# Three feature tiles converted half by half, and the first tile's slot matrix made by one full-width product

## The chip, the cores and the metric

The kernel runs on one core of a Trainium2 chip. The time is the device time of one execution in microseconds. Where several runs are given, it is their median. One execution of the kernel before was also profiled; its span goes from the first instruction to the last and is a little shorter than its own time.

## What is computed

Three layers follow each other on 4 batches of 576 tokens (2304 tokens, model width 512): local attention with 8 heads of 64, a soft mixture of experts with 32 slots, and a feed-forward layer of 2048 features with a gated rectifier. The change touches the end of the second and the beginning of the third:

```python
    slot_out[e] = h @ w2[e]            # the soft mixture, 32 slots of 512
    x = c @ slot_out                   # c: 2304 x 32, the share of each token in each slot
    h = x @ w_in
    g = np.maximum(h, 0.0) + alpha * np.minimum(h, 0.0)
    return g @ w_out
```

w_in and w_out arrive as 64-bit floats, which the kernel itself turns into 32-bit ones on the chip.

## The kernel before, in words

**The order of the third layer.** x is never formed. As h = c @ (slot_out @ w_in), the kernel first multiplies the 32 slot rows by w_in and keeps the result split into a rounded part and a remainder (mpack); a product with cpack, the tokens' shares in the same split form, then gives h. The 2048 features are cut into 16 tiles of 128, f = 0 to 15, the tokens into three blocks r of 768. The table VISITS names the order in which blocks and tiles meet: block 0 with tile 0, block 1 with tiles 0 and 1, block 2 with tiles 0 to 2, block 0 with tiles 1 to 3, and so on. One meeting of a block and a tile is a step s; steps 0, 1 and 3 use tile 0, step 2 is the first with tile 1, step 5 with tile 2, step 8 with tile 3. A visit's six accumulators y (one PSUM bank each for 128 tokens) are copied out or added to what earlier visits left.

**soT.** The slot rows end up transposed in PSUM (tile st). At line 843 one ScalarE copy moves them to soT, 128 x 4 x 32: for each of four blocks of 128 of the model width (k), the 32 slots. The planned order below begins right behind it.

**Converting a tile (conv, lines 779 to 804).** One DMA brings the two weights of a tile, 1 MB of 64-bit words; w_in lies in the first half of the columns, w_out in the second. Step 0 takes the absolute value of the upper words on ScalarE (line 786). Steps 1 and 2 clamp and shift (VectorE, lines 788 and 790, one input each). Steps 3 and 4 bring in the sign and the lowest bits (VectorE, lines 793 and 796, two inputs each). Step 4 also makes SP issue the load of the tile that comes four later (load_one, line 248), for f from 2 on. Step 5 rounds w_out to wo_hi, step 6 leaves the remainder as wo_lo (line 803). For f > 0 all of 1024 columns go through steps 0 to 4 at once, as tasks c0 to c4, and c5 and c6 are on ScalarE and VectorE. Tile 0 is done in two halves of 512: its w_in before the planned order starts, its w_out as tasks d0 to d4, then c5 and c6 on VectorE.

**From a tile to h (lines 889 to 973).** m1(f) (line 892) multiplies soT with the tile's w_in, four products of 32 columns packed side by side into PSUM, one for each k, so that the four partial sums stand in four groups of 32 partitions. ms copies them to SBUF on ScalarE (line 419, shown as q_m<-hb). m2 (line 969) is a product with the constant sel_s that adds the four groups and writes the sum four times below each other. mp (ScalarE, line 419, mpack<-hb) rounds it into mpack, and m3 (VectorE, line 897) puts the remainder into its lower half.

**A step.** For each of two halves i of a block: h (line 903, TensorE), relu (ScalarE, line 1007), gate (VectorE, line 911), ghs, the rounded copy (ScalarE, line 419), gls, the remainder (GpSimd, line 1013). Then 18 products y (line 917): for six groups of 128 tokens ghs with wo_hi, ghs with wo_lo, gls with wo_hi. Evictions of y are copies on ScalarE (line 419) or additions on VectorE (line 925).

**Who sets the order.** Each engine works through its own queue in program order. The tasks above are put in order by a planner written in the kernel (plan and schedule, lines 86 to 193): a list scheduler that takes the task that can start earliest, by a table of costs (COST), and at equal starts the one with the smallest key. The keys come from the place at which a tile is first used (when) less a LEAD for each kind of task; a randomised search over 1500 rounds shifts keys and keeps an order if its planned end is not later. A task can have an earliest time; for steps 0 to 4 of tiles 1 to 5 it is 2.6 f + 1.6 us. The tasks of a tile are made here:

```python
            task(("m1", f), "pe", lambda f=f: m1(f), [dep("c4", f), dep("ms", f - 1)], k - LEAD["m1"])
            task(("ms", f), "act", lambda f=f: copy("act", ms[:, f % 2], mb[0]), [("m1", f), dep("m2", f - 2)],
                 k - LEAD["ms"])
            task(("m2", f), "pe", lambda f=f: mm(mb[1], lhsT=sel_s, rhs=ms[:, f % 2], start=True, stop=True),
                 [("ms", f), dep("m3", f - 1)], k - LEAD["m2"])
```

Until the first y can start, TensorE is kept running with products that nobody reads (warm, line 501): 2, 4 and 6 of them behind m1(0), m2(0) and the second h.

Of the kernel before, what the change touches and what calls it, by code (L numbers as in the profile page):

```python
# [10 lines left out]
F32 = mybir.dt.float32  # L11
# [8 lines left out]
B, H, S, D = 4, 8, 576, 64  # L20
NT, DM, NS, DFF, NE, EF = 2304, 512, 32, 2048, 8, 1024
# [11 lines left out]
          (1, 12, NF), (2, 14, NF))  # L33
NEXT = {f: f + 4 for f in range(2, NF - 4)}
PRE = (4, 5)


PERIOD = 4.3
# [2 lines left out]
            relu=(0.39, 0.52), gate=(0.53, 0.64), gh=(0.42, 0.54), gl=(1.3, 1.35), ms=(0.17, 0.3), mp=(0.17, 0.3),  # L41
            m3=(0.3, 0.32), copy=(0.48, 0.62), add=(0.66, 0.72), c0=(1.05, 1.18), c1=(0.95, 1.0), c2=(0.95, 1.0),
            c3=(1.65, 1.75), c4=(1.5, 1.6), c5=(0.52, 0.64), c6=(1.25, 1.35),
            d0=(0.6, 0.7), d1=(0.44, 0.5), d2=(0.44, 0.5), d3=(0.75, 0.8), d4=(0.72, 0.8),
            q=(0.75, 2.9), k=(0.75, 2.9), qq=(1.45, 3.6), v=(1.5, 3.7), vh=(0.75, 2.95), w=(2.7, 4.9), sm=(0.215, 0.4), s=(0.96, 1.15), max=(0.67, 0.7), sub=(0.69, 0.72), exp=(0.56, 0.66),
            sum=(0.69, 0.72), rec=(0.42, 0.46), norm=(1.04, 1.1), t=(0.44, 0.7), pv=(0.96, 1.25),
# [7 lines left out]
FROUNDS = 1500  # L54
MODE = dict(sm=128, t=128, x=128, dT=128, s=64, pv=64, lt=32, part=32)
LAND = 3.5
LEAD = dict(h=15, relu=14, gate=10, gh=8, gl=2, m1=34, ms=32, m2=30, mp=26, m3=25, c0=70, c1=66, c2=62, c3=58, c4=50, c5=24,
            c6=14, warm=60, pb=8)
# [125 lines left out]
def tile_kernel(ctx, tc, qk, v, phi, w1, w2, w_f, alpha, mask, out):  # L184
    nc = tc.nc
# [39 lines left out]
    eps_s = const.tile([128, 1], F32, name="eps_s")  # L225

    slotT = keep.tile([128, 4, NS], F32, name="slotT")
    soT = keep.tile([128, 4, NS], F32, name="soT")
    rinv = keep.tile([128, 1], F32, name="rinv")
    lts = keep.tile([96, B, 192], F32, name="lts")  # L230


    plan = []
# [183 lines left out]
    def copy(eng, out, in_):  # L417
        if eng == "act":
            nc.scalar.copy(out=out, in_=in_)  # L419
        elif eng == "dve":  # L420
            nc.vector.tensor_copy(out=out, in_=in_)
        else:
            nc.gpsimd.tensor_copy(out=out, in_=in_)
# [183 lines left out]
    with tc.manual_schedule():  # L607
# [34 lines left out]
        b = B - 1  # L642
# [197 lines left out]
        warm(2, st[:, 256:384])  # L840
        emit_st()
        warm(2, st[:, 256:384])
        nc.scalar.copy(out=soT, in_=st[:, 0:4 * NS].rearrange("p (k s) -> p k s", k=4))
        ex.close()


# [37 lines left out]
        def task(name, engine, fn, need, key, kind=None, ready=0.0):  # L884

            need = [n for n in need if n is not None]
            tasks[name] = (engine, fn, need, key, *COST[kind or name[0]], ready)

        def m1(f):
            w = fbuf[f % 4]  # L890
            for g in range(4):
                mm(mb[0][32 * g:32 * g + 32, :], lhsT=soT[:, g, :], rhs=w[:, 128 * g:128 * g + 128], start=True,  # L892
                   stop=True, skip_group_check=True)

        def m3(f):
# [53 lines left out]
        def dep(*n):  # L949
            return n if n in tasks else None  # L950

        for f in range(NF):
            k = when[f]
            if f > 0:
                landed = [("c4", x) for x in NEXT if NEXT[x] == f and x > 0]
                for i in range(7):
                    need = {0: landed + [dep("c6", f - 4), dep("m1", f - 4)], 5: [("c4", f)], 6: [("c5", f)]}
                    task((f"c{i}", f), "act" if i in (0, 5) else "dve", lambda f=f, i=i: conv(f, i),
                         need.get(i, [(f"c{i - 1}", f)]), k - LEAD[f"c{i}"], f"c{i}",
                         2.6 * f + 1.6 if f < 6 else 0.0)  # L960
            else:
                for i in range(5):
                    task((f"d{i}", 0), "dve" if i else "act", lambda i=i: conv(0, i, 1), [dep(f"d{i - 1}", 0)], -40, f"d{i}")
                task(("c5", 0), "dve", lambda: conv(0, 5), [("d4", 0)], -40, "c5")
                task(("c6", 0), "dve", lambda: conv(0, 6), [("c5", 0)], -2, "c6", 3.0)
            task(("m1", f), "pe", lambda f=f: m1(f), [dep("c4", f), dep("ms", f - 1)], k - LEAD["m1"])
            task(("ms", f), "act", lambda f=f: copy("act", ms[:, f % 2], mb[0]), [("m1", f), dep("m2", f - 2)],
                 k - LEAD["ms"])
            task(("m2", f), "pe", lambda f=f: mm(mb[1], lhsT=sel_s, rhs=ms[:, f % 2], start=True, stop=True),
                 [("ms", f), dep("m3", f - 1)], k - LEAD["m2"])  # L970
            task(("mp", f), "act", lambda f=f: copy("act", mpack[:, 128 * f:128 * f + 128], mb[1]), [("m2", f)],
                 k - LEAD["mp"])
            task(("m3", f), "dve", lambda f=f: m3(f), [("mp", f)], k - LEAD["m3"])
        seen, last_y = {}, {}
# [23 lines left out]
        for s, (v, r, f) in enumerate(steps):  # L998
            for i in range(2):
                k = when[s, i]  # L1000
                task(("h", s, i), "pe", lambda s=s, i=i: h_(s, i), [("m3", f), dep("gate", s - 1, i)], k - LEAD["h"])
                if (s, i) == (0, 1):
                    for j, (after, m) in enumerate(((("m1", 0), 2), (("m2", 0), 4), (("h", 0, 1), 6))):
                        task(("warm", j), "pe", lambda m=m: (y[0, 5] is None and bank(0, 5), warm(m, y[0, 5][:, 0:128])),
                             [after], -LEAD["warm"], "warm%d" % m)
                task(("relu", s, i), "act",
# [9 lines left out]

        def place(name):

            return {"h": name[-1], "relu": name[-1], "gate": name[-1], "m1": 0, "ms": 0, "m2": 1, "mp": 1, "m3": 1}.get(name[0])

        schedule(tasks, place, lambda name, x: LAND if name[0] == "c0" and x[0] == "c4" else 0.0, rounds=FROUNDS, spread=(3, 10, 30))

# [56 lines left out]
```

## Time and profile before

| what | value |
|---|---|
| median of three runs | 381.15 us (380.51 to 381.78) |
| the profiled execution, its own time | 381.29 us |
| its span | 379.5 us |
| TensorE busy in the span | 360.5 us (95%) |
| VectorE busy | 267.7 us (71%) |
| ScalarE busy | 216.5 us (57%) |
| GpSimd busy | 159.7 us (42%) |
| chain that ended last, by engine | TensorE 68%, DMA 14%, VectorE 10%, ScalarE 4% |

The profile calls the engines PE (TensorE; PEld is its weight load), DVE (VectorE), ACT (ScalarE), POOL (GpSimd) and SP. A line gives the output and input tile; small helpers such as the copy at line 419 stand for many tasks, told apart by their tiles. Tiles are named by the memory they lie in: feature tiles in conversion are pt_m and e_m, their raw weights q_m, xs_m or v_m, and both PSUM banks of h and of the slot products are hb. The busy shares are means over stages with different limits: attention and the loads of the experts' weights come before 139 us and the third layer after.

### The profile page before, as it was taken

Reading aid. Unit: us, or ns where it says so; the run is one execution under the profiler, and the core shown is the slowest. Engines: PE = TensorE matmul, PEld = TensorE weight load, DVE = VectorE, ACT = ScalarE, POOL = GpSimd, SP = SyncE. Lnnn points to the kernel's source line nnn. Section 1 sums busy time; section 2 is a strip of 40 time slices with the busy share of each in tenths; the row PEclk is TensorE's granted clock in tenths of the full one; section 3 lists DMA queues with packets and bytes.
Section 4 is the critical chain, followed back from the end, with each engine's and each line's share of the span. In section 5 each row is a group of like instructions: output and inputs, shape, how many; then the busy total and the mean of one; then the engine's idle time right before and its main releaser. Section 6 shows DMA issues by size and latency. Waiting matters only on the chain.

```text
span 379.5 us, 7885 instructions
## 1 busy us (share of the span) xinstructions
PE 360.5 (95%) x3108; PEld 269.6 (71%) x3108; DVE 267.7 (71%) x450; ACT 216.5 (57%) x470; POOL 159.7 (42%) x141
## 2 busy tenths in 40 slices
PE   7699999899999988799999999999999999999995
PEld 4486786766444446578778778888778877888884
DVE  5979989875237449999999989899786225224263
ACT  3568977484123238967884956755557435535450
POOL 5347666320000004546554566664545434633550
PEclk9999999999899999999999999999999999999999
DMA  8999999999999994233232333020000000003246
GB/s 300 417 415 373 374 394 418 408 369 422 419 419 415 416 422 198 68 139 126 111 113 90 131 112 111 9 104 0 3 0 1 3 0 0 2 0 107 62 140 191
DMA packets 15044, 74.01 MB, mean 195 GB/s; under 512 B 1920, under 2 KB 2320, under 8 KB 8992
## 3 DMA queue, kind: packets, MB, share of 16 engines
q1 hardware_dynamic: 14032, 71.80, 48.6%
q10 hardware_dynamic: 912, 1.64, 1.2%
q8 instruction: 24, 0.39, 0.4%
q14 instruction: 12, 0.10, 0.1%
q0 software_dynamic: 64, 0.07, 0.1%
HBM read 68.79 MB, written 4.72 MB: 194 GB/s over the span
## 4 chain that ended last, share of the span: by engine, by line
PE 68%; DMA 14%; DVE 10%; ACT 4%; issue 2%; POOL 0%; ACTq 0%; DVEq 0%; SPq 0%; POOLq 0%
PE y L917 49%; DMA w<-w 8%; PE hb L903 4%; DMA q_m<-qk 3%; PE pv L403 2%; PE si L485 2%; PE s L355 2%; DVE e_m L369 2%; PE h L714 1%; PE x L476 1%; DMA m_m<-mask 1%; DMA q_m<-w_f 1%; PE hb L892 1%; DVE l L376 1%; DVE m L366 1%
## 5 line engine op out<-in xcount | busy, mean ns | idle before, releaser
L1013 POOL TENSOR_TENSOR gls<-gs,ghs 128x384 fp32r<-128x384 f32 x96 | 116.1, 1224 | 162.9 <-ACT ghs L419 112.0
L917 PE MATMUL y<-wo_hi,ghs 128*128 128x512 f32 x289 | 90.8, 397 | 1.2 <-ACT ghs L419 0.9
L911 DVE SCALAR_TENSOR_TENSOR gs<-gs,beta_s,hb 128x384 f32<-128x384 f32 x96 | 56.5, 609 | 49.2 <-ACT gs L1007 45.8
L917 PE MATMUL y<-wo_hi,gls 128*128 128x512 f32 x289 | 87.5, 392 | 1.1 <-POOL gls L1013 1.1
L917 PE MATMUL y<-wo_lo,ghs 128*128 128x512 f32 x289 | 88.4, 392 | 0.0
L1007 ACT ACTIVATE gs<-hb 128x384 f32<-128x384 f32 x96 | 44.9, 495 | 45.5 <-PE hb L903 39.0
L917 PEld LDWEIGHTS y<-wo_hi,gls 128*128 128x128 f32 x289 | 54.1, 188 | 13.0 <-POOL gls L1013 1.7
L917 PEld LDWEIGHTS y<-wo_hi,ghs 128*128 128x128 f32 x289 | 53.3, 188 | 13.5 <-ACT ghs L419 2.4
L419 ACT CAST ghs<-gs 128x384 fp32r<-128x384 f32 x96 | 48.9, 518 | 22.3 <-DVE gs L911 21.6
L917 PEld LDWEIGHTS y<-wo_lo,ghs 128*128 128x128 f32 x289 | 54.0, 188 | 10.3
L903 PE MATMUL hb<-cpack,mpack 128*128 128x384 f32 x96 | 29.2, 342 | 1.7 <-DVE mpack L897 1.1
L385 POOL TENSOR_TENSOR e_m<-e_m,l 128x512 f32<-128x512 f32 x18 | 19.1, 1066 | 27.1 <-DVE l L381 18.0
L355 PE MATMUL s<-q_m 128*64 128x64 f32 x576 | 20.9, 224 | 2.7 <-DMA q_m<-qk 1.5
L355 PEld LDWEIGHTS s<-q_m 128*64 128x64 f32 x576 | 18.7, 138 | 5.5 <-issue 2.1
L903 PEld LDWEIGHTS hb<-cpack,mpack 128*128 128x128 f32 x96 | 17.9, 188 | 6.3 <-DVE mpack L897 1.3
L403 PEld LDWEIGHTS pv<-pt_m,v_m 128*64 128x64 f32 x576 | 18.2, 138 | 5.7 <-issue 3.0
L403 PE MATMUL pv<-pt_m,v_m 128*64 128x64 f32 x576 | 20.4, 224 | 1.6 <-issue 1.3
L419 ACT COPY pt_m<-t 64x512 f32<-64x512 f32 x35 | 20.2, 578 | 2.3 <-PE t L390 1.8
L717 ACT ACTIVATE v_m<-h,rinv 128x256 f32<-128x256 f32 x8 | 3.8, 474 | 22.4 <-PE h L714 22.4
L372 ACT ACTIVATE e_m<-e_m 128x512 f32<-128x512 f32 x18 | 11.2, 629 | 7.7 <-DVE e_m L369 7.6
L788 DVE TENSOR_SCALAR pt_m<-pt_m 128x1024 f32<-128x1024 f32 (+1 forms) x9 | 9.8, 1083 | 8.1 <-ACT pt_m L786 8.1
L366 DVE TENSOR_REDUCE m<-s 128x8 f32<-128x512 f32 x18 | 12.1, 671 | 2.2 <-PE s L355 2.2
(164 smaller groups left out, 512.1 us busy)
## 6 DMA issues: line engine op xcount, KB each, us to landing
w<-w SPq DMA_DIRECT2D x23, 1024.0 KB, 10.8
q_m<-qk SPq DMA_DIRECT2D x13, 576.0 KB, 6.8
q_m<-w_f SPq DMA_DIRECT2D x7, 1024.0 KB, 4.9
v_m<-w_f SPq DMA_DIRECT2D x7, 1024.0 KB, 4.8
v_m<-v SPq DMA_DIRECT2D x12, 576.0 KB, 7.8
q_m<-w SPq DMA_DIRECT2D x4, 1024.0 KB, 13.2
v_m<-w SPq DMA_DIRECT2D x2, 1024.0 KB, 14.8
q_m<-qk SPq DMA_DIRECT2D x4, 288.0 KB, 5.2
```

Source lines behind the costliest of these rows:

```text
L355: mm(s[r:r + 64, col:col + 64], lhsT=q_of(u)[:, 2 * o:2 * o + 64], rhs=keys(u, c, x), start=False, stop=True, skip_group_check=True)
L366: nc.vector.tensor_reduce(out=m, in_=by_key(s_[g]), op=ALU.max, axis=AX.X)
L372: nc.scalar.activation(out=es[g % 4], in_=es[g % 4], func=AF.Exp, scale=SCALE)
L385: nc.gpsimd.tensor_tensor(out=e, in0=e, in1=bc(e_[g, "l"], 128, 8, 64), op=ALU.mult)
L403: mm(pv[hs, n], lhsT=vv[u % 4][:, c, hs], rhs=pts[:, NBS * (g % 2) + n, h], start=True, stop=True, skip_group_check=True)
L419: nc.scalar.copy(out=out, in_=in_)
L788: nc.vector.tensor_scalar(out=t, in0=t, scalar1=2.0 ** -15, scalar2=FMAX, op0=ALU.max, op1=ALU.min)
L903: mm(hb[i], lhsT=mpack[:, 128 * f:128 * f + 128], rhs=cpack[:, t0:t0 + 384], start=True, stop=True)
L911: nc.vector.scalar_tensor_tensor(out=g, in0=g, scalar=beta_s[:, f:f + 1], in1=hb[i], op0=ALU.mult, op1=ALU.add)
L917: mm(y[steps[s][0], t][:, sl], lhsT=g, rhs=wo_hl[p == 1][:, f, sl], start=start, stop=stop, skip_group_check=True)
L1007: lambda s=s, i=i: nc.scalar.activation(out=half(gs, s, i, 4), in_=hb[i], func=AF.Relu, scale=-1.0),
L1013: lambda s=s, i=i: nc.gpsimd.tensor_tensor(out=half(gls, s, i, 6), in0=half(gs, s, i, 4), in1=half(ghs, s, i, 6).bitcast(F32), op=ALU.subt ...
```

## The change

soT becomes 128 x 4 x 4 x 32, each group of 32 slots written four times side by side, by ScalarE for the first two k and by VectorE for the other two. It shares its memory with lts, which nobody reads any more by then. For tile 0, m1 is four products of full width that accumulate in one place, mb[1]; ms and m2 of tile 0 are gone, and mp reads m1's result. Tiles 1 to 3 go through steps 0 to 4 in two halves of 512 columns, tasks i0 to i4 for w_in and c0 to c4 for w_out, the latter with keys later by 10 and never ahead of the same step of the first half; m1 waits for i4 only. c5 and c6 work as before. The load of the tile four later hangs on the second half. c6 of tile 0 has a later key than before, and c5 of tile 0 too. The warming products behind m1(0) and m2(0) are now four behind m1(0).

```diff
+SPLIT = (1, 2, 3)
...
+            m10=(0.9, 1.0),
...
-    soT = keep.tile([128, 4, NS], F32, name="soT")
     rinv = keep.tile([128, 1], F32, name="rinv")
-    lts = keep.tile([96, B, 192], F32, name="lts")
+    lts_m = keep.tile([128, B * 192], F32, name="lts")
+    lts = lts_m[0:96].rearrange("p (b c) -> p b c", b=B)
+    soT = lts_m[:, 0:16 * NS].rearrange("p (k r s) -> p k r s", k=4, r=4)
...
-        nc.scalar.copy(out=soT, in_=st[:, 0:4 * NS].rearrange("p (k s) -> p k s", k=4))
+        so = st[:, 0:4 * NS].rearrange("p (k o s) -> p k o s", k=4, o=1)
+        for i, eng in enumerate(("act", "dve")):
+            k = slice(2 * i, 2 * i + 2)
+            copy(eng, soT[:, k], so[:, k].to_broadcast([128, 2, 4, NS]))
...
         def m1(f):
             w = fbuf[f % 4]
-            for g in range(4):
-                mm(mb[0][32 * g:32 * g + 32, :], lhsT=soT[:, g, :], rhs=w[:, 128 * g:128 * g + 128], start=True,
+            for g in range(4 * (f == 0)):
+                mm(mb[1], lhsT=soT[:, g].rearrange("p r s -> p (r s)"), rhs=w[:, 128 * g:128 * g + 128], start=(g == 0), stop=(g == 3))
+            for g in range(4 * (f > 0)):
+                mm(mb[0][32 * g:32 * g + 32, :], lhsT=soT[:, g, 0], rhs=w[:, 128 * g:128 * g + 128], start=True,
                    stop=True, skip_group_check=True)
...
             if f > 0:
-                landed = [("c4", x) for x in NEXT if NEXT[x] == f and x > 0]
-                for i in range(7):
...
+                landed = [("c4", x) for x in NEXT if NEXT[x] == f and x > 0] + [dep("c6", f - 4), dep("m1", f - 4)]
+                at = 2.6 * f + 1.6 if f < 6 else 0.0
+            for i in range(5):
+                if f in SPLIT:
+                    task((f"i{i}", f), "dve" if i else "act", lambda f=f, i=i: conv(f, i, 0), [(f"i{i - 1}", f)] if i else landed,
+                         k - LEAD[f"c{i}"], f"d{i}", at)
+                h = 1 if f == 0 or f in SPLIT else None
+                need = [(f"c{i - 1}", f)] if i else landed if f else []
+                task((f"c{i}", f), "dve" if i else "act", lambda f=f, i=i, h=h: conv(f, i, h),
+                     need + [dep(f"i{i}", f)], (k - LEAD[f"c{i}"] if f else -40) + 10 * (f in SPLIT), f"d{i}" if h else f"c{i}", at if f else 0.0)
+            for i in (5, 6):
+                task((f"c{i}", f), "act" if i == 5 and f else "dve", lambda f=f, i=i: conv(f, i), [(f"c{i - 1}", f)],
+                     k - LEAD[f"c{i}"] if f else -60 + 20 * i, f"c{i}", 0.0 if f or i == 5 else 3.0)
+            task(("m1", f), "pe", lambda f=f: m1(f), [dep("i4" if f in SPLIT else "c4", f) if f else None, dep("ms", f - 1)], k - LEAD["m1"],
+                 "m1" if f else "m10")
+            if f > 0:
+                task(("ms", f), "act", lambda f=f: copy("act", ms[:, f % 2], mb[0]), [("m1", f), dep("m2", f - 2)],
+                     k - LEAD["ms"])
...
-                    for j, (after, m) in enumerate(((("m1", 0), 2), (("m2", 0), 4), (("h", 0, 1), 6))):
+                    for j, (after, m) in enumerate(((("m1", 0), 4), (("h", 0, 1), 6))):
```

## Rows read from the trace of the kernel before

**Rows 1.** Stretches: length, busy PE, PEld, DVE, ACT, POOL (count); clock, DMA share, GB/s.
```profile
151.90:153.10 1.20, 0.30 (x3) 0.11 (x2) 0.64 (x2) 1.20 (x5) 0.00 (x0) 1.00 0.00 0
...
157.98:159.05 1.07, 0.02 (x2) 0.01 (x1) 1.07 (x3) 1.07 (x3) 1.07 (x2) 1.00 0.00 0
...
165.00:180.00 15.00, 15.00 (x74) 12.14 (x74) 14.74 (x17) 10.86 (x26) 8.19 (x6) 1.00 0.40 141
...
240.00:375.44 135.44, 135.43 (x649) 111.00 (x647) 76.67 (x111) 69.99 (x151) 63.58 (x57) 1.00 0.13 40
```

**Rows 2.** TensorE's waits from 139.3 to 166 us (total, times, longest).
```profile
PE y L917 <- POOL gls L1013: 1.1, 1, 1.1
PE y L917 <- ACT ghs L419: 0.9, 1, 0.9
```

**Rows 3.** ScalarE in order of time, 139 to 168 us (start, us, ...).
```profile
139.25 0.27 ACT L843 COPY soT<-st 128x128 f32<-128x128 f32 x1 [1.69 <-PE st L501]
139.42 0.68 ACT L786 ACTIVATE pt_m<-q_m 128x512 f32<-128x512 f32 x1
...
140.91 0.27 ACT L419 CAST mpack<-hb 128x128 fp32r<-128x128 f32 x1 [0.58 <-PE hb L969]
...
143.33 0.87 ACT L1007 ACTIVATE gs<-hb 128x384 f32<-128x384 f32 x2 [1.10 <-PE hb L903]
...
152.47 0.57 ACT L419 CAST ghs<-gs 128x384 fp32r<-128x384 f32 x1
...
163.12 1.16 ACT L786 ACTIVATE e_m<-q_m 128x1024 f32<-128x1024 f32 x1 [1.01 <-DMA q_m<-w_f]
```

**Rows 4.** TensorE in order of time, 139 to 181 us.
```profile
139.57 0.43 PE L892 MATMUL hb<-pt_m,soT 128*32 128x128 f32 x8 [0.35 <-ACT soT L843]
...
140.71 1.06 PE L501 MATMUL y<-eye_s 128*128 128x128 f32 x8
...
145.83 0.96 PE L917 MATMUL y<-wo_hi,ghs 128*128 128x512 f32 x3
...
150.35 0.43 PE L892 MATMUL hb<-pt_m,soT 128*32 128x128 f32 x8
...
177.76 0.43 PE L892 MATMUL hb<-e_m,soT 128*32 128x128 f32 x8
```

**Rows 5.** Groups of instructions by line and shape, 0 to 145 us: PSUM copies of 128x256.
```profile
L421 DVE COPY xt<-pv 128x256 f32<-128x256 f32 x4 | 1.6, 413 | 0.2 <-ACT xt L419 0.2
...
L419 ACT COPY xt<-pv 128x256 f32<-128x256 f32 x4 | 1.4, 371 | 0.0
```

**Rows 6.** VectorE in order of time, 139 to 180 us.
```profile
140.12 0.43 DVE L788 TENSOR_SCALAR pt_m<-pt_m 128x512 f32<-128x512 f32 x1 [4.14 <-ACT pt_m L786]
...
141.78 0.69 DVE L796 SCALAR_TENSOR_TENSOR pt_m<-q_m,pt_m 128x512 int32<-128x512 int32 x1
142.50 0.29 DVE L897 TENSOR_TENSOR mpack<-hb,mpack 64x128 fp32r<-64x128 f32 x1
...
143.90 0.69 DVE L788 TENSOR_SCALAR pt_m<-pt_m 128x1024 f32<-128x1024 f32 x1
144.61 0.61 DVE L911 SCALAR_TENSOR_TENSOR gs<-gs,beta_s,hb 128x384 f32<-128x384 f32 x1
...
148.40 1.51 DVE L796 SCALAR_TENSOR_TENSOR pt_m<-xs_m,pt_m 128x1024 int32<-128x1024 int32 x1
149.84 0.60 DVE L911 SCALAR_TENSOR_TENSOR gs<-gs,beta_s,hb 128x384 f32<-128x384 f32 x1
...
153.24 0.30 DVE L897 TENSOR_TENSOR mpack<-hb,mpack 64x128 fp32r<-64x128 f32 x1 [0.69 <-ACT mpack L419]
153.56 1.65 DVE L793 SCALAR_TENSOR_TENSOR e_m<-q_m,e_m 128x1024 int32<-128x1024 int32 x1
...
161.85 1.50 DVE L788 TENSOR_SCALAR pt_m<-pt_m 128x1024 f32<-128x1024 f32 x1
...
165.70 1.22 DVE L796 SCALAR_TENSOR_TENSOR e_m<-v_m,e_m 128x1024 int32<-128x1024 int32 x1
```

More of the change, by code (lines that the diff above doesn't have):

```diff
@@ L954, in tile_kernel @@
             if f > 0:
-                landed = [("c4", x) for x in NEXT if NEXT[x] == f and x > 0]
-                for i in range(7):
[L957 to L971, printed above, removed]
+                landed = [("c4", x) for x in NEXT if NEXT[x] == f and x > 0] + [dep("c6", f - 4), dep("m1", f - 4)]
@@ new lines, in tile_kernel @@
+            for i in (5, 6):
[6 more added lines that the diff above has]
+                     k - LEAD["ms"])
+                task(("m2", f), "pe", lambda f=f: mm(mb[1], lhsT=sel_s, rhs=ms[:, f % 2], start=True, stop=True),
+                     [("ms", f), dep("m3", f - 1)], k - LEAD["m2"])
@@ L972, in tile_kernel @@
+            task(("mp", f), "act", lambda f=f: copy("act", mpack[:, 128 * f:128 * f + 128], mb[1]), [("m2" if f else "m1", f)],
                  k - LEAD["mp"])
@@ L1017, in place @@
         def place(name):
-            return {"h": name[-1], "relu": name[-1], "gate": name[-1], "m1": 0, "ms": 0, "m2": 1, "mp": 1, "m3": 1}.get(name[0])
-        schedule(tasks, place, lambda name, x: LAND if name[0] == "c0" and x[0] == "c4" else 0.0, rounds=FROUNDS, spread=(3, 10, 30))
+            return {"h": name[-1], "relu": name[-1], "gate": name[-1], "m1": int(name[-1] == 0), "ms": 0, "m2": 1, "mp": 1, "m3": 1}.get(name[0])
+        schedule(tasks, place, lambda name, x: LAND if name[0] in ("c0", "i0") and x[0] == "c4" else 0.0, rounds=FROUNDS, spread=(3, 10, 30))
 FMAX = float(np.array([0x47EFFFFF], np.uint32).view(np.float32)[0])
```

## The prediction

> **What bounds the kernel now.** I read the chain of waits first. It runs through the weight DMA, then the small products of the soft mixture up to soT, then for 25 us through ScalarE, VectorE and their queues, and at the end through TensorE alone. The stretches say the same in busy time [rows 1]: from 165 us on TensorE is busy without a hole (15.00 us in 15.00, then 135.43 in 135.44) and its granted clock is 1.00, its upper level of 2.4 GHz. So nothing done there for VectorE or ScalarE can pay, and whatever is won earlier is kept to the end as long as those two stay ahead of TensorE. All that this change can win lies between soT and 165 us. There TensorE waits 1.1 us for a gls and 0.9 us for a ghs [rows 2], besides a fill ahead of the first y in which it mostly runs warming products. The stretches place the two waits: 151.9 to 153.1 us has 0.30 us of TensorE in 1.20, 157.98 to 159.05 us has 0.02 in 1.07 [rows 1]. VectorE is full all along (still 14.74 in the 15 us from 165), so its order decides; ScalarE, full for the whole of the first hole, is the second queue to watch.
>
> **soT in four copies, in two halves.** Today one ScalarE copy starts at 139.25 us, lasts 0.27, and the first m1 starts at 139.57, 0.05 behind its end [rows 3, 4]. A half writes 128x256. The nearest rows are copies of that size out of PSUM, 0.371 us on ScalarE and 0.413 on VectorE [rows 5]. VectorE is idle then: it waits 4.14 us for tile 0's Abs [rows 6]. The repeating read has no row: below, it costs what today's 128x128 does, nothing added; above, four of today's copies, 1.06 us, or 0.8 more. I take the 128x256 row, which has the same count of written elements. m1 then starts at 139.25 + 0.37 + 0.05 = 139.67, 0.1 late, and its third product, 0.5 later, finds VectorE's half ready since 139.66. Tile 0's second Abs is queued behind the copy on ScalarE; it starts 0.17 us into today's copy [rows 3] and would start some 0.1 later, and with it VectorE's four steps of tile 0.
>
> **m1 of tile 0 at full width, no ms and m2.** Today m1 runs as 8 packed instructions in 0.43 us, then come the ms copy and m2, and mp starts at 140.91, 1.34 us after m1 [rows 3, 4]. Four products of full width are eight instructions of 128x128 in fp32, and eight of these take 1.06 us in the warming row [rows 4]. So m1 ends at 139.67 + 1.06 = 140.73 and mp starts at 140.8: 0.1 us won. The Trainium skill ("TensorEngine Tiling (Array Packing)", Theoretical Speedup) gives a packing of 32 columns up to four times the speed, which speaks against giving it up here; the rows have 1.06 against 0.43, 2.5 times. By the full factor m1 would take 1.7 us and mp would come 0.5 us late.
>
> But m3, which needs mp, does not wait for it today. mp ends at 141.18; m3 starts at 142.50, right behind VectorE's fourth step of tile 0, begun at 141.78 [rows 3, 6]. The tenth won at mp is worth nothing unless m3 is put between the last steps. If it stays it is 0.1 us late by the later Abs; ahead of the last step it gains 0.7 - 0.1 = 0.6 us. I take nothing, with +0.1 and -0.6 as ends, because the steps of tile 0 keep the earlier keys in the planner.
>
> **The gate behind it.** The first gate starts at 144.61, though its relu, first of the two that begin at 143.33 and take 0.87 together, was through at about 143.8 [rows 3, 6]. In between VectorE does tile 1's first step over all 1024 columns, 0.69 us from 143.90. The planner bills tile 1's Abs on ScalarE at its full length (1.05) and not before 4.2 us, so it expects the relu behind it. Split, the Abs is billed 0.6 and VectorE's step takes 0.43 like tile 0's [rows 6], so the gate can go first (-0.7) or still second (-0.26). I take -0.5. The first y, today at 145.83 [rows 4], comes 0.5 us earlier.
>
> **Tile 1 in halves, w_in first.** Today tile 1's steps on VectorE run from 143.90 to the end of the 1.51 us one begun at 148.40, with three gates among them; its m1 follows at 150.35 [rows 4, 6]. m1 reads w_in only. Of these 6.0 us nearly half is w_out's, so m1 of tile 1 can start some 2.5 us earlier, and with it ms, m2, mp and m3, now at 153.24 [rows 6]. That m3 releases the h, relu, gate, ghs and gls of step 2, and the late gls is what TensorE waits for until 159.05. This 1.05 us goes: -1.0, ends 0 and -1.05. The ghs wait until 153.1 is another matter: its gate started at 149.84 behind the 1.51 us step, and the copy itself at 152.47 behind ScalarE's evictions of step 0 [rows 3, 6]. The halves let the gate in earlier; the evictions stay. I take -0.4 of the 0.9, ends 0 and -0.9. What is late next is the eviction of step 0's banks, which step 1's products have to wait for.
>
> **What the halves cost.** A half of the two scalar steps is 0.43 us against 0.69, a half of the two others 0.69 against 1.22 [rows 6]. Per tile (4 x 0.43 + 4 x 0.69) - (2 x 0.69 + 2 x 1.22) = 4.48 - 3.82 = 0.66 us on VectorE, 2.0 us for three tiles: the lower end. Some whole steps take longer beside GpSimd's work, 1.50 us for the same 0.69 and 1.65 for 1.22 [rows 6]; if each added step paid this 0.81 or 0.43, it would be 0.66 + 2 x 0.81 + 2 x 0.43 = 3.1 us a tile, the upper end. I take 1.0 a tile, nearer the first, since added steps also fall where GpSimd pauses. Cover for tile 1: ahead of step 2 VectorE idles 0.69 us at 153.24 and then does a 1.65 us step of tile 2 [rows 6], 2.3 us that TensorE doesn't need yet, so 1.0 is hidden. Cover for tiles 2 and 3: the last step of tile 3, begun at 165.70, ends at 166.92, and its m1 runs at 177.76 [rows 4, 6], so there are 10 us. Without this cover all of it is on the path. ScalarE pays 2 x 0.68 - 1.16 = 0.2 us a tile [rows 3], hidden where it waits for VectorE. The DMAs: SP issues the loads of tiles 6 and 7 behind the second half of tiles 2 and 3, 1 to 2 us later at most; ScalarE waited 1.01 us for tile 6 at 163.12 [rows 3], with an eviction queued behind it. I count this at nothing, with +0.5 as end. The warming products are 4 and 6 in place of 2, 4 and 6, all in the fill: nothing.
>
> **Sum.** -0.5 - 1.0 - 0.4 = -1.9 us. The profiled execution had 381.29 us (span 379.5, 1.8 around it); the median of the runs is 381.15, 0.14 less. 381.15 - 1.9 = 379.25, say 379.2.
>
> **Rivals.**
> *The order hides it.* The order of this stage is searched anew by a randomised planner. If it runs w_out's halves right behind w_in's, so that the halves don't do what they say, or if the evictions on ScalarE hold steps 1 and 2 wherever feature tile 1 stands, only the first gate's half microsecond is left: 380.6. For it: in the first hole ScalarE is busy for all of the 1.20 us [rows 1]. Against it: the larger wait comes from m3 of tile 1.
>
> *VectorE becomes the bound.* Its added 2 to 3 us land in the 25 us in which it is full already. It decides from the point where tile 1's w_out isn't through c5 and c6 when step 2's products begin. Steps 0 and 1 give TensorE 36 products, 7.3 us at the pace of [rows 1] (74 instructions in 15.00 us); in that time VectorE owes four gates, the second half and c6, 4 x 0.61 + 2.24 + 0.69 = 5.4 us, and w_in's half before them, 2.24. That is about even. If more steps are stretched by GpSimd, TensorE waits for the 2.0 us: 381.15 + 2.0 - 0.5 = 382.7. For it: VectorE's busy time, and steps of 1.5 us. Against it: the 2.3 us of cover above. The Trainium skill ("VectorE: DVE Perf Modes", The TRN2 errata) says that each instruction on SBUF data pays a fixed cost, and asks for tiles of 512 elements or more to spread it; the rows have that cost, 2 x 0.43 - 0.69 = 0.17 us for each added step.
>
> *All waits go.* m3 of tile 0 moves ahead of the last step, the gate goes first, and both later waits vanish: -0.6 - 0.7 - 0.9 - 1.05 = -3.25, so 377.9.
>
> **Chances.** Forecast 0.50, the order hides it 0.26, VectorE the bound 0.14, all waits go 0.10. A measurement of this kernel can tell about 0.3% (1.1 us) from no change. Faster than 380.0: 0.60; from there to 382.3: 0.26; slower: 0.14. The range reaches from the case of all waits to halfway into the slower one: 377.6 to 382.0. The forecast's own is 378.2 to 380.0.
>
> **What would show it.** Right: no ms and m2 of tile 0; its m1 near 1.06 us; the first y near 145.3; m1 of tile 1 near 148; no wait of TensorE for a gls near 159; TensorE without holes from 165 on and its end 1.9 us earlier. Wrong: a wait of TensorE for wo_hi, wo_lo or gs between 145 and 180 us (VectorE as the bound); holes as large as before, with evictions in them (the order hides it); any hole behind 165 us, which before doesn't have.

## The result and the profile after

The changed kernel takes 383.22 us (median of eight runs, 382.56 to 384.83), the kernel before 380.83 us in the same comparison. The ratio is 1.0077 with an interval of 1.0057 to 1.0097, so the change costs 2.4 us by the medians and 2.9 by the ratio, where 1.9 us of gain were forecast. The profiled execution had 382.65 us.

The first part of the page of the changed kernel gives the span and, for each engine, busy time, share of the span and instructions:

```profile
span 380.9 us, 7883 instructions
PE 359.6 (94%) x3100; PEld 268.2 (70%) x3102; DVE 275.9 (72%) x463; ACT 216.3 (57%) x472; POOL 158.7 (42%) x141
```

VectorE has 8.2 us more to do than the 267.7 us of before; the other engines have what they had. The prediction had given it 3.0 us more for twelve split steps.

**The front.** soT stands under the name of the memory that it shares, lts. It became ready in another place of the span than before (137.98 us here, 139.25 us there; the change leaves the instructions ahead of it alone, and over the profiled executions of this record, one for each kernel, its start lies anywhere from 137.98 to 140.43 us), so stages are compared from the start of the first soT copy. ScalarE, VectorE and TensorE of the changed kernel in order of time, three views:

```profile
137.98 0.37 ACT L422 COPY lts<-st 128x256 f32<-128x256 f32 x1 [1.70 <-PE st L504]
...
139.61 0.27 ACT L422 CAST mpack<-hb 128x128 fp32r<-128x128 f32 x1 [0.68 <-PE hb L898]
```

```profile
138.38 0.42 DVE L424 COPY lts<-st 128x256 f32<-128x256 f32 x1 [4.08 <-ACT lts L422]
...
140.61 0.29 DVE L905 TENSOR_TENSOR mpack<-hb,mpack 64x128 fp32r<-64x128 f32 x1
140.94 0.69 DVE L799 SCALAR_TENSOR_TENSOR pt_m<-q_m,pt_m 128x512 int32<-128x512 int32 x1
141.66 0.43 DVE L424 CAST wo_hi<-pt_m 128x512 fp32r<-128x512 f32 x1
142.12 0.69 DVE L806 TENSOR_TENSOR wo_lo<-pt_m,wo_hi 128x512 fp32r<-128x512 f32 x1
142.73 0.42 DVE L791 TENSOR_SCALAR pt_m<-pt_m 128x512 f32<-128x512 f32 x1
143.19 0.61 DVE L919 SCALAR_TENSOR_TENSOR gs<-gs,beta_s,hb 128x384 f32<-128x384 f32 x1
...
146.85 1.50 DVE L796 SCALAR_TENSOR_TENSOR pt_m<-xs_m,pt_m 128x512 int32<-128x512 int32 x1
...
151.06 1.24 DVE L793 TENSOR_SCALAR e_m<-e_m 128x512 int32<-128x512 int32 x1
152.33 0.29 DVE L905 TENSOR_TENSOR mpack<-hb,mpack 64x128 fp32r<-64x128 f32 x1
...
153.60 0.42 DVE L793 TENSOR_SCALAR e_m<-e_m 128x512 int32<-128x512 int32 x1
...
170.09 2.04 DVE L796 SCALAR_TENSOR_TENSOR pt_m<-v_m,pt_m 128x1024 int32<-128x1024 int32 x1
172.05 1.13 DVE L919 SCALAR_TENSOR_TENSOR gs<-gs,beta_s,hb 128x384 f32<-128x384 f32 x2
...
184.51 1.14 DVE L919 SCALAR_TENSOR_TENSOR gs<-gs,beta_s,hb 128x384 f32<-128x384 f32 x2
185.57 1.22 DVE L799 SCALAR_TENSOR_TENSOR pt_m<-q_m,pt_m 128x1024 int32<-128x1024 int32 x1
186.71 2.05 DVE L796 SCALAR_TENSOR_TENSOR e_m<-q_m,e_m 128x1024 int32<-128x1024 int32 x1
```

```profile
138.40 1.17 PE L898 MATMUL hb<-pt_m,lts 128*128 128x128 f32 x8 [0.46 <-ACT lts L422]
...
144.40 0.97 PE L925 MATMUL y<-wo_hi,ghs 128*128 128x512 f32 x3
...
146.30 0.97 PE L925 MATMUL y<-wo_hi,ghs 128*128 128x512 f32 x3 [0.76 <-ACT ghs L422]
147.20 0.42 PE L900 MATMUL hb<-pt_m,lts 128*32 128x128 f32 x8
...
152.68 0.62 PE L911 MATMUL hb<-cpack,mpack 128*128 128x384 f32 x2 [0.67 <-DVE mpack L905]
...
172.71 0.44 PE L911 MATMUL hb<-cpack,mpack 128*128 128x384 f32 x1 [0.55 <-DVE gs L919]
...
189.67 0.50 PE L925 MATMUL y<-wo_hi,gls 128*128 128x512 f32 x1 [1.21 <-POOL gls L1025]
```

The wide m1 of tile 0 takes 1.17 us, and mp starts 1.63 us after soT, 0.03 ahead of before (1.66, [rows 3]). m3 has moved ahead of the last step and comes 2.63 us after soT in place of 3.25 [rows 6]. m1 of tile 1 runs 9.2 us after soT in place of 11.1 [rows 4]. So the front and w_in first do what they are meant to do. But the first gate still waits behind c6 of tile 0 and tile 1's first half step (142.12 and 142.73), so the first y comes 6.42 us after soT in place of 6.57. Two rows show what is new: the same operation on the same 512 columns takes 0.42 us at 153.60 and 1.24 us at 151.06. The longer one holds up m3 of tile 1 (152.33), and TensorE waits 0.67 us for it (152.68).

**Where the time goes.** The starts of the products y, counted from soT, in both profiled executions:

| product y no. | before, us | after, us | after - before |
|---|---|---|---|
| 0 | 6.57 | 6.42 | -0.15 |
| 36 | 18.11 | 19.21 | +1.10 |
| 72 | 29.70 | 29.29 | -0.41 |
| 108 | 38.86 | 39.80 | +0.94 |
| 180 | 59.03 | 61.09 | +2.06 |
| end of TensorE | 236.17 | 239.05 | +2.88 |

At product 72 the changed kernel is ahead by 0.41 us: the late gls near 159 us [rows 2] is gone and what was lost at 36 is won back. Then it loses 2.5 us up to product 180, and 0.8 more up to the end. TensorE's waits of the changed kernel from 137.9 us to the end (total, times, longest):

```profile
PE hb L911 <- DVE gs L919: 1.9, 4, 0.9
PE y L925 <- POOL gls L1025: 1.2, 1, 1.2
PE hb L911 <- DVE mpack L905: 1.2, 2, 0.7
PE y L925 <- ACT ghs L422: 0.8, 1, 0.8
```

The stretches of the changed kernel (columns as in [rows 1]):

```profile
170.00:180.00 10.00, 9.45 (x49) 7.10 (x47) 10.00 (x12) 8.34 (x19) 5.43 (x4) 1.00 0.60 211
180.00:190.00 10.00, 8.79 (x46) 6.88 (x45) 9.76 (x12) 7.59 (x17) 6.42 (x5) 1.00 0.21 66
...
240.00:377.03 137.03, 136.76 (x653) 111.26 (x651) 81.69 (x113) 71.23 (x154) 65.10 (x58) 1.00 0.14 46
```

Before, TensorE had no hole from 165 to 180 us and none from 240 us on [rows 1]. Now 0.55, 1.21 and, behind 240 us, 0.27 us are missing, at a granted clock of 1.00, the upper of its two levels (2.4 GHz), as before. These three are 2.0 of the 3.3 us lost behind product 72; the rest is spread over short intervals and is not taken apart. The two large holes are the rows at 172.71 and 189.67. At 172.71 h waits for a gate (172.05) that stands behind a VectorE step of 2.04 us (170.09). At 189.67 y waits for a gls, and there it is GpSimd that is held up:

```profile
185.81 3.81 POOL L1025 TENSOR_TENSOR gls<-gs,ghs 128x384 fp32r<-128x384 f32 x2 [1.88 <-issue]
```

The y needs the second of these two, which ends at 189.62. Their gates were done by 185.65 (184.51), but beside VectorE's steps of 185.57 and 186.71 the two take 3.81 us; one that isn't held up takes 1.01, as at 149.50 (last section). All these steps are whole steps of tiles that the change doesn't split.

### The profile page after: what moved, and what is told of

Read it like the earlier page. It is cut to its first block, busy times and chain, and to the rows that moved or that the text cites. A ratio compares the mean times of both kernels' runs of the same rounds, so it can differ in the third digit from the quotient of the medians.

```text
span 380.9 us, 7883 instructions
## 1 busy us (share of the span) xinstructions
PE 359.6 (94%) x3100; PEld 268.2 (70%) x3102; DVE 275.9 (72%) x463; ACT 216.3 (57%) x472; POOL 158.7 (42%) x141
## 4 chain that ended last, share of the span: by engine, by line
PE 54%; DVE 23%; DMA 13%; ACT 4%; issue 3%; POOL 0%; ACTq 0%; DVEq 0%; SPq 0%; POOLq 0%
PE y L925 41%; DMA w<-w 9%; PE hb L911 4%; DMA q_m<-qk 3%; DVE gs L919 3%; DVE pt_m L796 3%; DVE e_m L372 2%; DVE pt_m L799 2%; DVE l L379 2%; DMA m_m<-mask 1%; PE pv L406 1%; DVE e_m L796 1%; DVE m L369 1%; DVE q_m L424 1%; PE x L479 1%
## 5 line engine op out<-in xcount | busy, mean ns | idle before, releaser
L925 PE MATMUL y<-wo_hi,gls 128*128 128x512 f32 x289 | 88.6, 393 | 1.2 <-POOL gls L1025 1.2
L925 PEld LDWEIGHTS y<-wo_lo,ghs 128*128 128x128 f32 x289 | 54.1, 188 | 11.1 <-issue 0.6
L911 PE MATMUL hb<-cpack,mpack 128*128 128x384 f32 x96 | 31.1, 352 | 3.2 <-DVE gs L919 1.9
L479 PE MATMUL x<-eye_s,xt 128*96 128x128 f32 x96 | 13.6, 277 | 0.1
```

The costliest lines, as they stand in the source:

```text
L479: tr(t[0:96, i, 128 * h:128 * h + 128], tokens(b, 2 * p + h, 192 * j + 96 * k, 96), eye_s)
L911: mm(hb[i], lhsT=mpack[:, 128 * f:128 * f + 128], rhs=cpack[:, t0:t0 + 384], start=True, stop=True)
L925: mm(y[steps[s][0], t][:, sl], lhsT=g, rhs=wo_hl[p == 1][:, f, sl], start=start, stop=stop, skip_group_check=True)
```

## The experiments

The first theories were: *the front* (M), the wide m1 or the two-engine copy costs time; *VectorE's time* (V), twelve more instructions are too much for a full engine; and *the order* (S), the search happened on a bad one, or before on a lucky one. After the first kernels came *the bill*: the planner bills the halves too low and builds an order that is too tight. What speaks for it is in the code: the whole steps 1 to 4 have costs of 0.95, 0.95, 1.65 and 1.5 us in its table, the halves are billed as d1 to d4 (0.44, 0.44, 0.75, 0.72), about what tile 0's steps take before GpSimd has work in this layer (0.43 and 0.69). Per tile it books 4.7 us for eight halves against 5.05 us for four whole steps: it believes that halving saves time. "Search" below is the planner's randomised search. Where an order is "written out", the kernel has the list of tasks as a literal (ORDER) and no search. The edits are shown in part; "..." marks what is left out. Each expectation is given as it was written before its kernel ran.

**The front alone.** Before's order written out, with soT in four copies and the wide m1; no steps split.

```diff
+ORDER = (
...
-SPLIT = (1, 2, 3)
+SPLIT = ()
...
-        schedule(tasks, place, ...)
+        for n in json.loads(zlib.decompress(base64.b85decode(ORDER))):
+            tasks[tuple(n)][1]()
```

> Queue orders of before, written out; only soT in four copies and the full-width m1 of tile 0 without ms and m2; no halves for tiles 1 to 3. Theory V (the halves overload VectorE): within 0.3% of before, some 380.3 to 381.3 us, because m3 of tile 0 keeps its place behind the last conversion step. Rival M (the new front costs: two copies one behind the other, the wide product): 1.5 us or more above before. Rival S (the search found a bad order): like before.

Measured: 381.97 us, ratio 1.0026 (1.0004 to 1.0048), a little above the expected 380.3 to 381.3; from soT to the end of TensorE 236.37 us against 236.17. So the front costs 0.2 us of path; the rest of the difference between the two profiled executions lies ahead of soT. The interval of the time reaches 1.8 us, so it is the path that speaks against the first theory's 1.5 us.

**The halves alone, in the old order.** Before with each step of tiles 1 to 3 replaced by its two halves, one right behind the other, so that nothing comes earlier.

```diff
+SPLIT = (1, 2, 3)
...
+                for i in range(5 * (f in SPLIT)):
+                    task((f"i{i}", f), ..., lambda f=f, i=i: conv(f, i, 0), ...)
...
-                    task((f"c{i}", f), ..., lambda f=f, i=i: conv(f, i),
+                    task((f"c{i}", f), ..., lambda f=f, i=i: conv(f, i, 1 if f in SPLIT and i < 5 else None),
...
-        schedule(tasks, place, ...)
+        for n in json.loads(zlib.decompress(base64.b85decode(ORDER))):
+            tasks[tuple(n)][1]()
```

> Queue orders of before, written out; only the ten half steps of tiles 1 to 3 in place of the five whole ones, w_out's half right behind w_in's, so that m1 comes no earlier. It prices the halves alone. Theory V: VectorE's steps take 2 us more or up to 8 where GpSimd's work stretches each of them, and the time is 1.5 to 4 us above before. Rivals M and S: within 0.6 us of before.

Measured: 383.83 us, 1.0070 (1.0048 to 1.0093); the end of TensorE 2.1 us later. VectorE's steps 1 to 4 and c6 of all tiles add up to 95.4 us after soT against 93.1. The price falls early: 1.07 us by product 36, 2.04 by 72, nothing more after that. TensorE's waits of this kernel from 140 us on:

```profile
PE y L972 <- ACT xs_m L474: 1.6, 1, 1.6
PE hb L958 <- DVE mpack L952: 1.1, 1, 1.1
PE y L972 <- ACT ghs L474: 0.9, 1, 0.9
PE hb L1026 <- ACT q_m L474: 0.6, 1, 0.6
PE y L972 <- POOL gls L1070: 0.6, 1, 0.6
```

The longest wait, for an eviction on ScalarE (xs_m), begins at a load. Step 4 of tile 2 ends 2.0 us later after soT than before, and the load of tile 6 is issued behind it; ScalarE stands waiting for this load, with the eviction queued behind:

```profile
166.34 1.13 ACT L841 ACTIVATE e_m<-q_m 128x1024 f32<-128x1024 f32 x1 [1.95 <-DMA q_m<-w_f]
```

Before, ScalarE waited 1.01 us there and TensorE 0.2. So the halves make VectorE late, and most of what that costs here comes by way of a load, which the prediction had counted at nothing, with 0.5 us as its end. In the changed kernel ScalarE waits for no weights behind soT, and at product 72 it is ahead: its loss lies elsewhere.

**The new order with whole steps.** The changed kernel's order written out, a whole step in the place of each w_in half.

```diff
-SPLIT = (1, 2, 3)
+SPLIT = ()
...
-        schedule(tasks, place, ...)
+        for n in json.loads(zlib.decompress(base64.b85decode(ORDER))):
+            tasks[tuple(n)][1]()
```

> Queue orders of the changed kernel, written out, with the new front, but whole steps of tiles 1 to 3 in the places that w_in's halves have there, w_out's halves taken out. Theory V: VectorE gets back what the halves cost, and the time is between 1.5 us below before and 0.5 above. Rival S: the order itself is bad, and the time stays 2 to 3 us above before. Rival M: 1.5 us or more above before.

Measured: 384.36 us, 1.0083 (1.0052 to 1.0114). TensorE's waits of this kernel from 138 us on, the first three:

```profile
PE hb L964 <- DVE gs L972: 1.8, 2, 1.5
PE y L978 <- POOL gls L1078: 1.3, 1, 1.3
PE hb L953 <- DVE pt_m L852: 0.7, 1, 0.7
```

V expected the loss to go with the halves; it stays. Part of this says little, since an order made for halves must fit whole steps badly: m1 of tile 1 now waits 0.7 us for its last step. But the wait for a gls stands in the place of that of the changed kernel (52.0 us after soT here, 51.7 there), with two gls beside the same two whole steps, and no half is left to blame there. So this hole belongs to the order, by what it puts side by side.

**Another seed for the search.** The changed kernel and the kernel before, each with seed 2 in the search of the third layer's order alone.

```diff
-             ..., counts=lambda name: True):
+             ..., counts=lambda name: True, seed=1):
...
-    rng, succ = random.Random(1), {n: [] for n in tasks}
+    rng, succ = random.Random(seed), {n: [] for n in tasks}
...
-        schedule(tasks, place, ..., spread=(3, 10, 30))
+        schedule(tasks, place, ..., spread=(3, 10, 30), seed=2)
```

> The changed kernel with another seed for the search of the third layer's order. Theory V: slower than before with any seed, 382 to 385 us. Rival S: luck of the search, anywhere from 378 to 384 us. Rival M: 382 us or more.

> The kernel before, unchanged but for another seed of the search of the third layer's order. It asks whether the order of before is worth something by itself. Theory V (the halves and their load on VectorE make the loss): 380 to 382 us. Rival S (any newly searched order loses against that of before): 382 to 385 us.

Measured: 383.41 us for the changed kernel (1.0066, 1.0041 to 1.0091), 381.65 us for the kernel before (1.0017, 0.9993 to 1.0040). The loss is not one unlucky order, and the order of before is not a lucky one. The second order shows more: VectorE's steps and c6 add up to 93.1 us in it, as in the kernel before, and it loses as much as the first, in which they add up to 101.2. So the sum of VectorE's time alone does not make the loss.

**Fewer halves.** The changed kernel with no tile split, and with tile 1 alone.

```diff
-SPLIT = (1, 2, 3)
+SPLIT = ()            # the other kernel: (1,)
```

> The changed kernel without halves (SPLIT empty), its order searched anew with seed 1: new front alone, free order. Theory V: 380.5 to 382 us, since with the old order it was 0.9 us above before and a search may win half a microsecond. Rival S: 382.5 to 385 us.

> The changed kernel with halves for tile 1 alone, order searched. Theory V: a third of the added steps, so about 1 us above the kernel with the new front and no halves, 381 to 382.5 us. Rival S: no relation to the number of halves, 382 to 385 us.

Measured: none split 388.40 us (1.0195, 1.0167 to 1.0222), tile 1 alone 382.95 us (1.0052, 1.0033 to 1.0070). Neither is where V had it, and the first is above S too. The first has no halves at all and is the slowest, which the halves can't explain. It is 6.1 us late at product 72 and 6.8 at the end of TensorE, and the same work in before's order (the first experiment) has 381.97, so the search ended in a bad order. The search adds a spread of its own, and a version has to be judged by several orders. Tile 1 alone, in one order, costs two thirds of what all three cost (0.52% of 0.77%), not the third that V expected.

**The halves billed at what they take.** The changed kernel with costs for the halves from the means of its own trace (steps 1 to 4 of tiles 1 to 3: 0.63, 0.69, 1.0, 0.73).

```diff
-            m10=(0.9, 1.0),
+            m10=(0.9, 1.0), b0=(0.66, 0.75), b1=(0.63, 0.68), b2=(0.69, 0.74), b3=(1.0, 1.05), b4=(0.73, 0.78),
...
-                         k - LEAD[f"c{i}"], f"d{i}", at)
+                         k - LEAD[f"c{i}"], f"b{i}", at)
...
-                     ..., f"d{i}" if h else f"c{i}", at if f else 0.0)
+                     ..., f"c{i}" if h is None else f"b{i}" if f else f"d{i}", at if f else 0.0)
```

> The changed kernel, whose planner is given for the half steps of tiles 1 to 3 what they took on the chip on average (0.63, 0.69, 1.0 and 0.73 us) in place of tile 0's undisturbed 0.44, 0.44, 0.75 and 0.72. Theory V in the form that the planner loads VectorE by 4 us more than it knows: 381 to 382 us, 1 to 2.5 below the changed kernel. Rival S: no better than the changed kernel, 382.5 to 385 us.

> The changed kernel with the half steps billed as they were measured, and seed 2 in the search. Theory V (the planner loads VectorE by more than it knows): again better than the changed kernel with the same seed (383.4 us), 380.5 to 382.2 us. Rival S (the first billed order was luck): 382.5 to 385 us.

Measured: 381.04 us (0.9986, 0.9956 to 1.0016), and with seed 2 381.90 us (1.0020, 1.0001 to 1.0038). Both are where V had them. The instructions are the same, only their order is another, and the loss is gone. TensorE's waits of the first of the two from 138 us on:

```profile
PE hb L911 <- DVE gs L919: 0.8, 2, 0.6
PE y L925 <- ACT ghs L422: 0.6, 2, 0.4
...
PE y L925 <- POOL gls L1025: 0.2, 1, 0.2
```

The four waits for a gate (1.9 us) have become two (0.8), the 1.2 us for a gls has become 0.2.

**Is it GpSimd that lengthens the steps?** Both kernels with their own orders, in which gls is computed for 16 of its 384 columns only and the rest set to zero once; the remainder part of g is left out for the other 368.

```diff
+        nc.gpsimd.memset(gls.bitcast(F32), 0.0)
...
-    ... nc.gpsimd.tensor_tensor(out=half(gls, s, i, 6), in0=half(gs, s, i, 4), ...
+    ... nc.gpsimd.tensor_tensor(out=half(gls, s, i, 6)[:, 0:16], in0=half(gs, s, i, 4)[:, 0:16], ...
```

> The changed kernel, its queue orders unchanged; GpSimd computes gls for 16 of 384 columns only, the rest is zero (the remainder of g is left out of the product). GpSimd is then nearly idle. Theory V: VectorE's half steps take 0.42 and 0.68 us and whole ones 0.68 and 1.21, TensorE's waits ahead of h go, and the time falls by 3 to 6 us, below that of the kernel before with the same cut, since the order was planned for such durations. Rival S: it stays 2 to 3 us above the kernel before with the same cut.

> The kernel before with the same cut of gls. Theory V: it falls too, as its waits for gls and its stretched steps go, but by less, 1.5 to 3 us, to 378 to 379.5 us, and ends above the changed kernel with the cut. Rival S: it keeps its lead of 2 to 3 us over it.

Measured: the changed kernel 378.78 us (0.9944, 0.9921 to 0.9967), the kernel before 380.49 us (0.9986, 0.9968 to 1.0004). The sign is turned: with GpSimd nearly idle the changed kernel is 1.7 us faster than the kernel before under the same condition, with the same orders, and near the -1.9 that the prediction had worked out. Two things besides VectorE's steps take part in this. A gls itself is ready sooner, 0.22 us where nothing holds it up in place of 1.01, and the hole at 189.67 was a wait for one. And the kernel before gains less than the expected 1.5 to 3 us, because TensorE now waits 0.9 us for an eviction (0.2 before): ScalarE comes to the Abs of tile 6 1.1 us sooner after soT, but its load lands only 0.6 us sooner.

```profile
163.44 1.12 ACT L786 ACTIVATE e_m<-q_m 128x1024 f32<-128x1024 f32 x1 [1.57 <-DMA q_m<-w_f]
```

So it is shown that GpSimd's work turns the sign, but not how much of that is VectorE's steps. Groups of VectorE's instructions by line and shape, 141 to 176 us, first of the changed kernel, then of the one with the short gls:

```profile
L793 DVE TENSOR_SCALAR e_m<-e_m 128x512 int32<-128x512 int32 x4 | 3.3, 830 | 0.0
L791 DVE TENSOR_SCALAR e_m<-e_m 128x512 f32<-128x512 f32 x4 | 2.9, 738 | 0.0
L796 DVE SCALAR_TENSOR_TENSOR pt_m<-xs_m,pt_m 128x512 int32<-128x512 int32 x2 | 2.6, 1288 | 0.0
...
L796 DVE SCALAR_TENSOR_TENSOR pt_m<-v_m,pt_m 128x1024 int32<-128x1024 int32 x1 | 2.0, 2037 | 0.0
```

```profile
L793 DVE TENSOR_SCALAR e_m<-e_m 128x512 int32<-128x512 int32 x4 | 1.7, 428 | 0.0
L791 DVE TENSOR_SCALAR e_m<-e_m 128x512 f32<-128x512 f32 x4 | 1.6, 424 | 0.0
...
L796 DVE SCALAR_TENSOR_TENSOR pt_m<-xs_m,pt_m 128x512 int32<-128x512 int32 x2 | 1.4, 680 | 0.0
...
L796 DVE SCALAR_TENSOR_TENSOR pt_m<-v_m,pt_m 128x1024 int32<-128x1024 int32 x1 | 1.2, 1218 | 0.0
```

Halves that average 0.83 us beside a full gls take 0.43 without, and the whole step ahead of the hole at 172.71 takes 1.22 in place of 2.04. So here the halves take what the order was billed for. VectorE's steps and c6 after soT add up to 72.6 us in the changed kernel and 70.8 in the kernel before: 1.8 us more, near the 2.0 that the prediction had from undisturbed durations. With the full gls it is 101.2 against 93.1.

**Longer searches, and the old m1.** To see how much of all this is the search, four kernels had an order written out that a longer search had found: the changed kernel's halves with the measured costs, the same with its own costs, the kernel before, and the measured costs with the old soT, m1, ms and m2. The last was also run with the short search.

```diff
-        schedule(tasks, place, ...)
+        for n in json.loads(zlib.decompress(base64.b85decode(ORDER))):
+            tasks[tuple(n)][1]()
```

> The changed kernel's tasks with the half steps billed as measured, and an order from a much longer search (tens of thousands of rounds, best of several seeds), written out. Theory V: with the right bill a better plan is a better kernel: 378.5 to 380.5 us, under both kernels. Rival S: no relation, 381 to 385 us.

> The same tasks and the same long search with the changed kernel's own bill (halves as in tile 0, undisturbed). Theory V: the plan gains nothing on the chip, 382 to 385 us, 2 us or more above the billed order of the same search. Rival S: within 1 us of it.

> The tasks of the kernel before with the long search, so that the halves are compared with no halves at equal search. Theory V: 380.5 to 381.7 us, as the short search had come close to the same plan; 1 us or more above the billed halves. Rival S: anywhere.

> Halves billed as measured, but soT, m1, ms and m2 of tile 0 as before: the new front taken out. Theory V: the new front is worth little, so within 1 us of the billed kernel with it, 380 to 382 us. Rival M (the front costs): 1 us or more below it, under 380 us. Rival S: 382 to 385 us.

> Halves billed as measured with soT, m1, ms and m2 of tile 0 as before, long search. It asks whether the 388 us of the short search belonged to these tasks or to a search that was stuck. Theory V: stuck; 379.5 to 381.5 us. Rival M' (without the wide product the halves can't pay): 384 us or more.

Measured, with the runs above:

| kernel | ratios of the orders tried |
|---|---|
| no halves, old front | 1 (seed 1), 1.0017 (seed 2), 1.0020 (long) |
| halves, costs as in the change | 1.0077 (seed 1), 1.0066 (seed 2), 1.0073 (long) |
| halves, costs as measured | 0.9986 (seed 1), 1.0020 (seed 2), 1.0031 (long) |
| the same with the old m1 | 1.0190 (seed 1), 1.0018 (long) |

Two kernels with the full gls are not in the table: the first experiment (no halves, new front, before's order, 1.0026) and the same tasks searched anew (1.0195). A longer search doesn't help against wrong costs: 383.99 us. Nor does it with right ones: 382.37 us, 1.6 less (2 or more were expected), where 378.5 to 380.5 were expected, and that is no less than the 381.96 of no halves, where it was to be 1 us less. In the second and third line the two bills don't overlap, three orders of each. But with the old m1 a search with the right bill ended at 1.0190, in none of the places expected, so the bill is not all that makes an order good. The old m1 with the long search has 381.40 us, as expected, so those 388.24 were again an order that was bad, not the m1. With right costs the halves are worth nothing that these runs can show: no version beats the kernel before clearly.

## Why the prediction was wrong

**What bounds the kernel** held: TensorE, with VectorE full until well past 165 us. "whatever is won earlier is kept to the end as long as those two stay ahead of TensorE" was the condition, and VectorE did not stay ahead; nor did GpSimd, which the condition doesn't name.

**soT and m1 of tile 0** were costed right in their sum (mp "0.1 us won", measured 0.03), but not in their parts. The prediction found VectorE's half ready in time because VectorE is idle; the row at 138.38 shows it starting when ScalarE's half ends (137.98 + 0.37), with ScalarE's copy as its releaser. It ends at 138.80, and m1, begun at 138.40, takes 0.11 us more than the 1.06 of the warming row. m3 took the lower end, 0.6 us earlier, where nothing was taken.

**The gate** gained 0.15 us at the first y in place of 0.5. It came out by the smaller of the two cases, "still second (-0.26)": tile 1's first half step goes first, behind c6 of tile 0, which keeps the place that it had. So what m3 won is lost again at the gate, whose relu was through at 141.93, 1.3 us before it.

**Tile 1 in halves** was right in mechanism: m1 of tile 1 came 1.9 us earlier (2.5 predicted), and the gls wait near 159 us went. But product 72 starts 0.41 us ahead, where all of the 1.9 was to be won by then. Besides the gate, the 0.4 us of the ghs wait did not come (0.76 us in place of 0.9, at another place, 146.30), and the 0.67 us for m3 of tile 1 are new.

**What the halves cost** is the step that failed, and in it the cover. The sum had this cost at nothing, by "I take 1.0 a tile, nearer the first, since added steps also fall where GpSimd pauses" and "Cover for tiles 2 and 3: ... so there are 10 us." In its place the runs showed 3.3 us lost behind product 72, 1.8 of them in two holes: a gate behind a step of 2.04 us, and two gls that took 3.81 us beside VectorE's steps. The cost was mis-sized first. Added up from VectorE's timeline, the twelve whole steps of tiles 1 to 3 took 13.7 us and the 24 halves 18.3: 4.6 us, 1.5 a tile. Of before's twelve, five were stretched, by 2.3 us together; of the 24 halves eight, by 5.1 us. The undisturbed share is 1.8 us, near the 2.0 predicted. The rest is GpSimd's, and the short gls shows it by taking it away. What VectorE's steps do to GpSimd in turn, 1.9 us for a gls that otherwise takes 1.01, has no term in the prediction.

The larger fault is the cover. The ten microseconds stood in the old order; the planner, which believes that halves cost less than whole steps, made a new one without them. With the costs as measured the same 24 halves take 18.0 us, hardly less, and VectorE's steps and c6 after soT 97.1 (93.1 before, 101.2 in the changed kernel); that kernel's TensorE ends 235.7 us after soT, before's 236.2. With seed 2 they take 100.9, and its TensorE ends 1.1 us later than before's, where that of the changed kernel ends 2.9 later. So most of 4 to 8 us more of VectorE's time can be hidden by an order that expects them. How the bill of the halves leads to the two holes is not shown: the steps in them are whole ones, with other entries (1.65 for the 2.04 us), and a gls is billed 1.3 us in every version. That the changed kernel also has the other tiles' steps and c6 stretched by 3.5 us more than before was not taken apart further. A planner that knows GpSimd's place in time was not tried.

**Rivals.** *VectorE becomes the bound*, with 0.14 of the chance, came nearest, but neither in its place nor by its reckoning: it was to decide where step 2's products begin, for want of tile 1's w_out, and priced at +1.5 us (382.7). There, at product 36, the changed kernel is indeed 1.1 us behind, but TensorE waits for no wo_hi or wo_lo, and by product 72 it is ahead; the loss that stays is 2.4 to 2.9 us and comes after that, in its largest hole from GpSimd. Its sign, a wait for gs between 145 and 180 us, came (0.55 us at 172.71), and so did the sign that was given to no rival, "any hole behind 165 us". *The order hides it* and *all waits go* did not happen.

What stays open is why two of the short searches ended 1.9% behind; only that they did, and that another order of the same tasks doesn't, is shown.

## What to carry to other kernels

Before work is cut into smaller instructions on an engine that shares something with another, look for rows of the same shape with two durations, and price the new instructions by the share that will meet the other engine: here 8 of 24 halves were stretched, by 0.63 us on average. Where a planner sets the order, a change of the tasks is also a change of the cost table: check each entry, new or old, against the trace in the stretch in which it will run, since an entry taken from a quiet stretch can make an order that has no slack where it is needed. Cover that is read from the old order is not a reserve if the order is made anew.

## What the hardware showed that was not expected

Beside a gls of GpSimd, a conversion step of VectorE takes its own time or up to 0.82 us more, whatever its size: 512 columns 0.42 or 1.24, 1024 columns 0.68 or 1.50 [rows 6], with two inputs 0.68 or 1.50 and 1.22 or 2.04. Every stretched step of the changed kernel overlaps a gls. An addition that doesn't grow with the size is paid per instruction, and halving doubles the instructions that can be hit. The gate, which reads its product from PSUM, takes 0.60 or 0.61 us in every row of one gate between 141 and 195 us. The Trainium skill ("SBUF — State Buffer", Who interferes with whom) says that VectorE and GpSimd share a pair of ports as an exclusive lock for a whole instruction, and that a VectorE instruction with at most one SBUF input, outside its two-port modes, is free of it. The gate's rows agree with the second. Steps 1 and 2 have one input and are stretched; whether they run in such a mode no row shows. With the first the trace agrees in so far as both sides lose time; the largest addition, 0.82 us, stays below the 1.01 us that the subtraction lasts when it isn't held up, as at 149.50 in these rows of GpSimd's timeline of the changed kernel:

```profile
146.33 1.47 POOL L1025 TENSOR_TENSOR gls<-gs,ghs 128x384 fp32r<-128x384 f32 x1 [0.89 <-ACT ghs L422]
149.50 1.01 POOL L1025 TENSOR_TENSOR gls<-gs,ghs 128x384 fp32r<-128x384 f32 x1 [1.70 <-ACT ghs L422]
```

So it works both ways: the gls begun at 146.33 us, beside the 1.50 us step of 146.85, lasts 1.47 us, and the two from 185.81 on, shown above, 1.9 us each.
